# Moving transposes, a parameter copy and the skip term inside a fused state-space and gated feed-forward kernel

## The chip, the core and the metric

The kernel runs on one core of a Trainium2 chip. The metric is the device time of one execution in microseconds (us), the median of several runs. A core has a matrix engine (TensorE, PE in the profile), a vector engine (VectorE, DVE), a scalar engine (ScalarE, ACT), a general engine (GpSimd, POOL) and a queue engine that mainly issues transfers (SyncE, SP). SBUF is the on-chip memory; PSUM is the small memory into which TensorE writes.

## What is computed

Input x has 2048 tokens (rows) of 512 features. After a layer norm there are two branches. One is a linear recurrence over tokens with 512 complex states, plus a skip term `x * Dskip`; the other is a gated feed-forward network. The result joins them with x:

```python
xn = _layernorm(x)
# branch A: complex diagonal recurrence, 512 states
Lam_bar = exp(dt * Lam);  B_bar = ((Lam_bar - 1.0) / Lam)[:, None] * Bmat
Bu = einsum("bld,pd->blp", xn + 0j, B_bar)
h_t = Lam_bar * h_{t-1} + Bu_t                   # for each token t
s = 2.0 * einsum("blp,dp->bld", h, Cmat).real + xn * Dskip
# branch B: feed-forward, inner width 1376
g = silu((gelu(xn @ w_gate) * (xn @ w_up)) @ w_down)
return x + s * g
```

## The kernel before

The 2048 tokens are cut into four slabs (s = 0 to 3) of 512 tokens, and a slab into four tiles (m = 0 to 3) of 128. For TensorE, x must lie with its features on the partitions: this transposed, normalised x is `xnT`. For slab 0 it comes from TensorE transposes and VectorE copies, for the later slabs from a transposing transfer on the SP queue. The complex recurrence is turned into real scans by rotating with tables of cosines and sines (`cos_b`, `sin_b`), which the kernel builds from the parameters at the start.

The start, in program order. `BT` is B transposed, with ri = 0 the real and ri = 1 the imaginary half; `pv` holds the parameters as rows, `pf` as columns:

```python
def b_transposes(ri):
    for k0 in range(0, KT, 2):                       # KT = 4
        tb = psum.tile([P, 2, D], BF16, name="tb_ps", tag="ps")
        ... # 8 TensorE transposes of Bn into tb
        ACT(out=BT[:, ri, k0 : k0 + 2, :], in_=tb[:, :, :], func=AF.Copy)

dummies(12)                                          # matmuls on zeros, to wake the clock
b_transposes(0)
... # statistics of tiles 0..3 on VectorE; their power -0.5 on GpSimd
xs = [norm0(0), norm0(1)]                            # VectorE
tps = [t_xn0(0, xs[0]), t_xn0(1, xs[1])]             # 4 TensorE transposes each
nc.tensor.transpose(pt_ps[:, :], pv[:, :], ident[0:16, 0:16])
b_transposes(1)
nc.vector.tensor_copy(out=pf[:], in_=pt_ps[:, :])    # parameter copy
nc.gpsimd.tensor_tensor(out=dt_[:], in0=euler[:], in1=ldt, op=ALU.pow)
xs += [norm0(2), norm0(3)]
... # copy tps[0], tps[1] into xnT
tps += [t_xn0(2, xs[2]), t_xn0(3, xs[3])]
... # copy tps[2], tps[3] into xnT
... # angles from pf and dt_, sines on ScalarE, tables on VectorE
```

Each slab then has its input products `u_ps` (copied to `U` by ScalarE), a chain of rotations and scans on VectorE that gives `hst`, eleven feed-forward tiles (`ffn`), and four down products (`down`):

```python
def u_pair(s, h, first=None):                        # a pair of state tiles, h = 0, 1
    for q in range(H2):                              # H2 = 2
        for ri in range(2):
            ... # 4 matmuls over kt of BT[:, ri, kt, pt] and xnT into u_ps
            ACT(out=U[:, ri, q, :], in_=u_ps[:, :], func=AF.Copy)

def y_mm(s, m, hst):
    ... # 8 matmuls of hst and C2 into y_ps
    for kt in range(0 if (s, m) in zs else KT):      # skip term as 4 matmuls with diagI
        nc.tensor.matmul(y_ps[:, kt * P : (kt + 1) * P], lhsT=xnT[:, kt, mg : mg + P],
                         rhs=diagI[:, kt, :], start=False, stop=(kt == KT - 1))

def epi(s, m, y_ps, g2):
    def f():                                         # VectorE
        y = y_ps
        if (s, m) in zs:
            y = work.tile([P, D], FP32, name="yt", tag="tt", bufs=3)
            TT(out=y[:], in0=y_ps[:, :], in1=zs[s, m][:], op=ALU.add)
        TT(out=yg[:], in0=y[:, :], in1=g2[:], op=ALU.mult)
        TT(out=ot[:], in0=yg[:], in1=x_tok[:, s * M + m, :], op=ALU.add)
    dve(now() + 0.3, 0.95, f)
    nc.sync.dma_start(out=out_td[mg : mg + P, :], in_=ot[:])
```

`zs` holds, for the first three tiles of the last slab, the skip term already multiplied on VectorE. `ln_out` makes the normalised tile of the next slab, starts its transposing transfer, and for the last slab also that product:

```python
def ln_out(s, m):
    ACT(out=xn[:], in_=x_tok[:, s * M + m, :], func=AF.Identity, scale=..., bias=...)
    nc.sync.dma_start_transpose(out=xnT[:, :, c0 : c0 + P], in_=xn[:])
    if s == NS - 1 and m < M - 1:
        skip(s, m, xn, now() + 1.5)                  # z = xn * Db on VectorE
```

The last tile of all is written in two halves of 256 columns (`y_halves`). The order of the VectorE instructions is not the plain program order: the helpers `dve`, `later` and `flush` keep an estimated clock for TensorE and VectorE while the program is built, and put long VectorE work between the urgent pieces by it.

Of the kernel before, what the change touches and what calls it, by code (L numbers as in the profile page):

```python
# [10 lines left out]
AF = mybir.ActivationFunctionType  # L11
ALU = mybir.AluOpType
FP32 = mybir.dt.float32
BF16 = mybir.dt.bfloat16
# [5 lines left out]
def kernel(  # L20
# [17 lines left out]
    nc = tc.nc  # L38
    P = 128
    S = 2048  # L40
    D = 512
    F = 1376
    KT = D // P
    NPT = 4
    H2 = NPT // 2
    TS = 512
    NS = S // TS
    M = TS // P
# [7 lines left out]
    TT = nc.vector.tensor_tensor  # L56
    TSC = nc.vector.tensor_scalar
    STT = nc.vector.scalar_tensor_tensor
    ACT = nc.scalar.activation
# [4 lines left out]
    consts = ctx.enter_context(tc.tile_pool(name="consts", bufs=1))  # L64
    work = ctx.enter_context(tc.tile_pool(name="work", bufs=2))
    psum = ctx.enter_context(tc.tile_pool(name="psum", bufs=8, space=bass.MemoryType.PSUM))
# [7 lines left out]
    wu = consts.tile([P, KT, F], BF16, name="wu")  # L74
    wd = consts.tile([P, NFT, D], BF16, name="wd")
    BT = consts.tile([P, 2, KT, D], BF16, name="BT")
    Db = consts.tile([P, D], BF16, name="Db")
    C2 = consts.tile([P, 2, NPT, D], BF16, name="C2")
    pv = consts.tile([16, P], BF16, name="pv")
    at0 = work.tile([P, NFT, TS], BF16, name="at", tag="at")  # L80
    Bn = work.tile([P, 2, NPT, D], BF16, name="Bn", tag="at")
# [18 lines left out]
    for i, (a, b) in enumerate(zip(cuts[:-1], cuts[1:])):  # L100
        nc.sync.dma_start(out=wg[:, :, a:b], in_=wg_r[:, :, a:b])
        nc.sync.dma_start(out=wu[:, :, a:b], in_=wu_r[:, :, a:b])
        if i == 2:
            nc.sync.dma_start(out=Db[:], in_=A_Dskip.unsqueeze(0).to_broadcast([P, D]))
        if i == 0:
            nc.sync.dma_start(out=x_tok[:, M : 2 * M, :], in_=x_r[:, M : 2 * M, :])
    nc.sync.dma_start(
        out=wd[:, 0 : NFT - 1, :], in_=B_w_down[0 : (NFT - 1) * P, :].rearrange("(k p) d -> p k d", p=P)
# [10 lines left out]
    ident = consts.tile([P, P], BF16, name="ident")  # L119
# [10 lines left out]
    euler = consts.tile([P, NPT], FP32, name="euler")  # L130
# [6 lines left out]
    def dummies(n):  # L137
        w_ps = psum.tile([P, TS], FP32, name="w_ps", tag="ps")
        for _ in range(n):
            nc.tensor.matmul(w_ps[:, :], lhsT=warm[:, 0:P], rhs=warm[:], start=True, stop=True)  # L140

    def b_transposes(ri):
        for k0 in range(0, KT, 2):
            tb = psum.tile([P, 2, D], BF16, name="tb_ps", tag="ps")
            for k in range(2):
                for pt in range(NPT):
                    nc.tensor.transpose(
                        tb[:, k, pt * P : (pt + 1) * P], Bn[:, ri, pt, (k0 + k) * P : (k0 + k + 1) * P], ident[:]
                    )
            ACT(out=BT[:, ri, k0 : k0 + 2, :], in_=tb[:, :, :], func=AF.Copy)  # L150

    st = consts.tile([P, NS, M, 6], FP32, name="st")
    mv = consts.tile([P, NS, M, 2], FP32, name="mv")
# [21 lines left out]
    def t_xn0(m, xn):  # L175
        tp = psum.tile([P, KT, P], BF16, name="tp", tag="ps")
        for kt in range(KT):
            nc.tensor.transpose(tp[:, kt, :], xn[:, kt * P : (kt + 1) * P], ident[:])
        return tp

    pf = consts.tile([P, 16], FP32, name="pf")
# [6 lines left out]
    ch = consts.tile(W3, BF16, name="ch")  # L188


    dummies(12)
    b_transposes(0)
    for a in (0, 2):
        for m in (a, a + 1):
            bn(0, m)
# [4 lines left out]
    tps = [t_xn0(0, xs[0]), t_xn0(1, xs[1])]  # L200
    pt_ps = psum.tile([P, 16], BF16, name="pt_ps", tag="ps")
    nc.tensor.transpose(pt_ps[:, :], pv[:, :], ident[0:16, 0:16])
    b_transposes(1)
    nc.vector.tensor_copy(out=pf[:], in_=pt_ps[:, :])
    nc.gpsimd.tensor_tensor(out=dt_[:], in0=euler[:], in1=ldt, op=ALU.pow)
    xs += [norm0(2), norm0(3)]
    for m in range(2):
        nc.vector.tensor_copy(out=xnT[:, :, m * P : (m + 1) * P], in_=tps[m][:, :, :])
    tps += [t_xn0(2, xs[2]), t_xn0(3, xs[3])]
    for m in range(2, 4):  # L210
        nc.vector.tensor_copy(out=xnT[:, :, m * P : (m + 1) * P], in_=tps[m][:, :, :])
    STT(out=thn[:], in0=lim, scalar=1.0 / (2.0 * math.pi), in1=dt_[:], op0=ALU.mult, op1=ALU.mult)
    TT(out=a1[:], in0=lre, in1=dt_[:], op=ALU.mult)
    nc.gpsimd.tensor_tensor(out=rho[:], in0=euler[:], in1=a1[:], op=ALU.pow)
# [54 lines left out]
            TSC(out=diagI[:, kt, :], in0=ident_f[:], scalar1=dsk[:, kt : kt + 1], scalar2=None, op0=ALU.mult)  # L269

    def fold_c(pt):
        tA = work.tile([P, D], FP32, name="tA", tag="tt", bufs=3)
        tB = work.tile([P, D], FP32, name="tB", tag="tt", bufs=3)
        ACT(out=tA[:], in_=CT[:, 1, pt, :], func=AF.Copy, scale=cim[:, pt : pt + 1])
        ACT(out=tB[:], in_=CT[:, 0, pt, :], func=AF.Copy, scale=cim[:, pt : pt + 1])
        dve(now() + 0.8, 0.66, lambda: STT(
            out=C2[:, 0, pt, :], in0=CT[:, 0, pt, :], scalar=cre[:, pt : pt + 1], in1=tA[:],
            op0=ALU.mult, op1=ALU.subtract,
        ))
        dve(now() + 1.6, 0.66, lambda: STT(  # L280
            out=C2[:, 1, pt, :], in0=CT[:, 1, pt, :], scalar=ncre[:, pt : pt + 1], in1=tB[:],
            op0=ALU.mult, op1=ALU.subtract,
        ))
# [6 lines left out]
    def now():  # L290
        return clk["pe"]
# [17 lines left out]
    def dve(ready, cost, f, late=0.8):  # L309
        drain(ready, late)  # L310
        clk["dve"] = max(clk["dve"], ready) + cost
        f()
# [12 lines left out]
    def u_pair(s, h, first=None):  # L325
        cols = slice(s * TS, (s + 1) * TS)
        i = 2 * s + h - U_BUFS
        flush(("u", i // 2, i % 2))
        U = work.tile([P, 2, H2, TS], BF16, name="U", tag="U", bufs=U_BUFS)
        for q in range(H2):  # L330
            pt = h * H2 + q
            for ri in range(2):
                u_ps = psum.tile([P, TS], FP32, name="u_ps", tag="ps")
                for kt in range(KT):
                    nc.tensor.matmul(  # L335
                        u_ps[:, :], lhsT=BT[:, ri, kt, pt * P : (pt + 1) * P], rhs=xnT[:, kt, cols],
                        start=(kt == 0), stop=(kt == KT - 1),
                    )
                pe_takes(KT)
                ACT(out=U[:, ri, q, :], in_=u_ps[:, :], func=AF.Copy)  # L340
                if first is not None:
                    first()
                    first = None
        return U
# [103 lines left out]
    def y_mm(s, m, hst):  # L448
        m0 = m * P
        mg = s * TS + m0  # L450
        for h in range(2):
            flush(("h", s, h))
        y_ps = psum.tile([P, D], FP32, name="y_ps", tag="ps")
        for j in range(2 * NPT):
            nc.tensor.matmul(  # L455
                y_ps[:, :], lhsT=hst[:, j // NPT, j % NPT, m0 : m0 + P], rhs=C2[:, j // NPT, j % NPT, :],
                start=(j == 0), stop=((s, m) in zs and j == 2 * NPT - 1),
            )
        for kt in range(0 if (s, m) in zs else KT):
            nc.tensor.matmul(  # L460
                y_ps[:, kt * P : (kt + 1) * P], lhsT=xnT[:, kt, mg : mg + P], rhs=diagI[:, kt, :],
                start=False, stop=(kt == KT - 1),
            )
        pe_takes(2 * NPT + 1)
        return y_ps

    def epi(s, m, y_ps, g2):
        mg = s * TS + m * P
        yg = work.tile([P, D], BF16, name="yg", tag="yg")
        ot = work.tile([P, D], BF16, name="ot", tag="ot")  # L470

        def f():
            y = y_ps
            if (s, m) in zs:
                y = work.tile([P, D], FP32, name="yt", tag="tt", bufs=3)
                TT(out=y[:], in0=y_ps[:, :], in1=zs[s, m][:], op=ALU.add)  # L476
            TT(out=yg[:], in0=y[:, :], in1=g2[:], op=ALU.mult)
            TT(out=ot[:], in0=yg[:], in1=x_tok[:, s * M + m, :], op=ALU.add)

        dve(now() + 0.3, 0.95, f)  # L480
        nc.sync.dma_start(out=out_td[mg : mg + P, :], in_=ot[:])
# [21 lines left out]
            TT(out=ot[:, c], in0=yg[:, c], in1=x_tok[:, s * M + m, c], op=ALU.add)  # L503
            (nc.sync, nc.scalar)[i].dma_start(out=out_td[mg : mg + P, c], in_=ot[:, c])

    zs = {}

    def skip(s, m, xn, ready):
        zs[s, m] = work.tile([P, D], BF16, name="z", tag="z", bufs=3)
        dve(ready, 0.34, lambda: TT(out=zs[s, m][:], in0=xn[:], in1=Db[:], op=ALU.mult))  # L510


    sx = consts.tile([P, NS, 2, M], FP32, name="sx")
    mq = consts.tile([P, NS, M], FP32, name="mq")
# [18 lines left out]
    def ln_out(s, m):  # L533
        xn = work.tile([P, D], BF16, name="xn", tag="xn", bufs=4)
        ACT(out=xn[:], in_=x_tok[:, s * M + m, :], func=AF.Identity, scale=rs[:, s, m : m + 1], bias=nb[:, s, m : m + 1])  # L535
        c0 = s * TS + m * P
        nc.sync.dma_start_transpose(out=xnT[:, :, c0 : c0 + P], in_=xn[:])
        if s == NS - 1 and m < M - 1:
            skip(s, m, xn, now() + 1.5)


    for ri, src in enumerate((A_C_re, A_C_im)):
# [31 lines left out]
    for s in range(NS):  # L574
# [20 lines left out]
        if s < NS - 1:  # L595
# [4 lines left out]
            for m in range(M):  # L600
                g2s[s, m] = down(s, m, ats[s])
    s = NS - 1
    for m in range(M):
        g2s[s, m] = down(s, m, ats[s])
        if m > 0:
            epi(s, m - 1, y_mm(s, m - 1, hsts[s]), g2s[s, m - 1])
    y_halves(s, M - 1, hsts[s], g2s[s, M - 1])


# [28 lines left out]
```

## Time and profile before

The median of three runs is 190.83 us (190.41 to 191.14). The profiled execution has a span of 188.8 us. Cut into stages by the starts of the slabs' input products and of the last down products, it looks like this (busy us of each engine):

| stage, us from the start | length | PE | DVE | ACT |
|---|---|---|---|---|
| start, to the first input product: 0 to 10.55 | 10.55 | 7.65 | 6.52 | 4.83 |
| slab 0: 10.55 to 36.91 | 26.36 | 25.90 | 24.43 | 24.92 |
| slab 1: 36.91 to 80.30 | 43.39 | 43.18 | 39.83 | 31.55 |
| slab 2: 80.30 to 124.70 | 44.40 | 43.01 | 41.78 | 28.98 |
| slab 3, to its down products: 124.70 to 168.09 | 43.39 | 43.11 | 38.57 | 23.77 |
| the end: 168.09 to 188.80 | 20.71 | 16.62 | 7.79 | 2.43 |

(Down products and y of a slab lie partly in the next stage.) A time in the profile is counted from the start of the span. "L335" is line 335 of the kernel before. In a group or timeline line, "out<-in" names the tile written and the tiles read, xN is the number of instructions merged in the line, and a bracket at the end gives the idle time of that engine ahead of the instruction and what ended it. [...] consecutive matmuls overlap in the records: what counts is the distance between their starts.

### The profile page before, as it was taken

The numbers are of one execution on the slowest core, as the hardware profiler recorded it, in microseconds if no ns is written. First come the engines' busy times: TensorE is split into PE (matmuls) and PEld (weight loads), VectorE is DVE, ScalarE is ACT, GpSimd is POOL, SyncE is SP. The second block draws the span as 40 slices with busy tenths as digits, with TensorE's granted clock in tenths as the row PEclk, the third lists the DMA queues.
The fourth block names the chain that finished last, engine by engine and source line by source line (L and its number), as shares of the span: only waits on it lengthen the run. The fifth ranks groups of instructions, "written<-read, shape, count | busy, mean of one in ns | idle before, by whom it ended". The sixth has DMA issues, their size and how long they took to land.

```text
span 188.8 us, 2554 instructions
## 1 busy us (share of the span) xinstructions
PE 179.5 (95%) x888; PEld 85.4 (45%) x905; DVE 158.9 (84%) x275; ACT 116.5 (62%) x209; POOL 20.3 (11%) x35
## 2 busy tenths in 40 slices
PE   7789999999999999999999999979999999999991
PEld 2544444444444444544444444534444444444451
DVE  4699699999998599999999977999999999540544
ACT  3489999997269969257259939727529644352110
POOL 3567200000000340000000180000000000000000
PEclk9999999999999999999999999999999999999999
DMA  5999977700000013200000003111000000000001
GB/s 153 316 371 361 224 141 220 145 3 0 0 0 0 0 23 91 56 28 28 3 2 0 0 2 83 40 47 56 0 0 0 3 0 27 28 28 31 28 30 56
DMA packets 21292, 12.39 MB, mean 66 GB/s; under 512 B 11456, under 2 KB 21280, under 8 KB 21280
## 3 DMA queue, kind: packets, MB, share of 16 engines
q1 hardware_dynamic: 21104, 12.16, 23.8%
q8 instruction: 7, 0.11, 0.3%
q10 hardware_dynamic: 176, 0.07, 0.1%
q14 instruction: 5, 0.04, 0.1%
HBM read 7.51 MB, written 2.10 MB: 51 GB/s over the span
## 4 chain that ended last, share of the span: by engine, by line
PE 76%; DVE 8%; ACT 6%; DMA 6%; issue 1%; SPq 1%; DVEq 0%; ACTq 0%
PE f_ps L440 20%; PE g_ps L420 15%; PE up_ps L425 15%; PE y_ps L455 13%; PE u_ps L335 11%; DMA Bn<-in_A_B_im_dram 3%; DMA xnT<-xn 3%; ACT U L340 2%; PE y_ps L460 1%; DVE at L433 1%; ACT ca L323 1%; ACT ub L432 1%; DVE Wt L358 1%; ACT L430 1%; DVE t__256 L569 1%
## 5 line engine op out<-in xcount | busy, mean ns | idle before, releaser
L425 PE MATMUL up_ps<-xnT,wu 128*128 128x512 bf16 (+1 forms) x172 | 44.8, 379 | 0.3
L420 PE MATMUL g_ps<-xnT,wg 128*128 128x512 bf16 (+1 forms) x174 | 44.7, 379 | 0.1
L440 PE MATMUL f_ps<-wd,at 128*128 128x512 bf16 (+1 forms) x174 | 38.9, 379 | 0.2
L430 ACT ACTIVATE gt<-g_ps 128x512 bf16<-128x512 f32 (+1 forms) x44 | 26.0, 592 | 10.6 <-PE g_ps L420 8.2
L335 PE MATMUL u_ps<-xnT,BT 128*128 128x512 bf16 x124 | 27.9, 379 | 2.3 <-DMA xnT<-xn 1.5
L384 DVE TENSOR_TENSOR_SCAN Ft<-rho,it,Wt 128x512 bf16<-128x512 f32 x24 | 30.0, 1272 | 0.0
L432 ACT ACTIVATE ub<-up_ps 128x512 bf16<-128x512 f32 (+1 forms) x44 | 26.3, 597 | 4.1 <-PE up_ps L425 3.7
L455 PE MATMUL y_ps<-C,hst 128*128 128x512 bf16 x115 | 27.8, 379 | 0.2
L445 ACT ACTIVATE g<-f_ps 128x512 f32<-128x512 f32 x16 | 9.6, 597 | 28.6 <-PE f_ps L440 28.6
L425 PEld LDWEIGHTS <-wu 128*128 128x128 bf16 (+1 forms) x176 | 17.6, 100 | 20.4
L440 PEld LDWEIGHTS <-at 128*128 128x128 bf16 (+1 forms) x176 | 17.2, 98 | 20.6
L420 PEld LDWEIGHTS <-wg 128*128 128x128 bf16 (+1 forms) x176 | 17.2, 100 | 18.4
L340 ACT ACTIVATE U<-u_ps 128x512 bf16<-128x512 f32 x32 | 17.9, 600 | 9.9 <-PE u_ps L335 9.9
L433 DVE TENSOR_TENSOR at<-gt,ub 128x512 bf16<-128x512 bf16 (+1 forms) x44 | 18.1, 415 | 6.9 <-ACT ub L432 6.6
L335 PEld LDWEIGHTS <-BT 128*128 128x128 bf16 x128 | 12.3, 98 | 17.0 <-issue 2.1
L455 PEld LDWEIGHTS <-hst 128*128 128x128 bf16 x120 | 11.7, 98 | 14.1
L535 ACT ACTIVATE xn<-x_tok,nb,rs 128x512 bf16<-128x512 bf16 x12 | 9.7, 812 | 4.5 <-POOL nb L531 4.5
L525 POOL TENSOR_SCALAR sx<-sx 128x4 f32<-128x4 f32 x2 | 2.2, 1115 | 83.9 <-ACT junk L520 83.9
L358 DVE TENSOR_TENSOR Wt<-pp,qq 128x1024 bf16<-128x1024 bf16 x16 | 10.6, 688 | 0.3
L358 DVE TENSOR_TENSOR hst<-pp,qq 128x1024 bf16<-128x1024 bf16 x16 | 10.6, 687 | 0.2
L520 ACT ACTIVATE junk<-x_tok 128x512 bf16<-128x512 bf16 x16 | 10.1, 630 | 0.3
L476 DVE TENSOR_TENSOR yt<-y_ps,z 128x512 f32<-128x512 f32 x3 | 2.1, 691 | 9.7 <-PE y_ps L455 9.7
(112 smaller groups left out, 171.7 us busy)
## 6 DMA issues: line engine op xcount, KB each, us to landing
out_dram<-ot SPq DMA_DIRECT2D x15, 128.0 KB, 1.7
x_tok<-in_A_x_dram SPq DMA_DIRECT2D x3, 512.0 KB, 5.8
wd<-in_B_w_down_dram SPq DMA_DIRECT2D x1, 1280.0 KB, 11.0
Bn<-in_A_B_re_dram SPq DMA_DIRECT2D x1, 512.0 KB, 4.3
Bn<-in_A_B_im_dram SPq DMA_DIRECT2D x1, 512.0 KB
wg<-in_B_w_gate_dram SPq DMA_DIRECT2D x1, 512.0 KB
wu<-in_B_w_up_dram SPq DMA_DIRECT2D x1, 512.0 KB, 8.4
wg<-in_B_w_gate_dram SPq DMA_DIRECT2D x1, 480.0 KB
```

The source lines that it names most:

```text
L335: nc.tensor.matmul(u_ps[:, :], lhsT=BT[:, ri, kt, pt * P : (pt + 1) * P], rhs=xnT[:, kt, cols], start=(kt == 0), stop=(kt == KT - 1),)
L340: ACT(out=U[:, ri, q, :], in_=u_ps[:, :], func=AF.Copy)
L358: return lambda: TT(out=dst()[i], in0=box["pp"][:, i, :, :], in1=box["qq"][:, 1 - i, :, :], op=op)
L384: nc.vector.tensor_tensor_scan(out=box["F"][:, ri, q, :], data0=rho[:, pt : pt + 1].to_broadcast([P, TS]), data1=box["W"][:, ri, q, :], in ...
L420: nc.tensor.matmul(g_ps[:fs, :], lhsT=wg[:, kt, fsl], rhs=xnT[:, kt, cols], start=(kt == 0), stop=(kt == KT - 1))
L425: nc.tensor.matmul(u_ps[:fs, :], lhsT=wu[:, kt, fsl], rhs=xnT[:, kt, cols], start=(kt == 0), stop=(kt == KT - 1))
L430: ACT(out=gt[:fs], in_=g_ps[:fs, :], func=AF.Gelu_apprx_tanh)
L432: ACT(out=ub[:fs], in_=u_ps[:fs, :], func=AF.Copy)
L433: dve(now() + 0.9, 0.34, lambda: TT(out=at[:fs, j, :], in0=gt[:fs], in1=ub[:fs], op=ALU.mult))
L440: nc.tensor.matmul(f_ps[:, :], lhsT=at[:fs, k, m0 : m0 + P], rhs=wd[:fs, k, :], start=(k == 0), stop=(k == NFT - 1))
L455: nc.tensor.matmul(y_ps[:, :], lhsT=hst[:, j // NPT, j % NPT, m0 : m0 + P], rhs=C2[:, j // NPT, j % NPT, :], start=(j == 0), stop=((s, m) ...
L520: ACT(out=junk[:], in_=x_tok[:, s * M + m, :], func=f, accum_out=sx[:, s, i, m : m + 1])
```

## The change

The change does five things. B's imaginary half is transposed in two parts around the transposes of the second half of x, so that x is not queued behind all of it. In each pair of input products, both real ones come first, so that the imaginary half of `BT` is needed later. On VectorE the norms of tiles 2 and 3 and the copies into `xnT` go ahead of the parameter copy. Ten dummy matmuls stand in place of twelve. And the VectorE version of the skip term in the last slab is taken out: its products `z`, its additions `yt` and the load of `Db` go, and all tiles use the four TensorE products with `diagI`. With that, y of the last slab's tile 0 is put ahead of the four down products, tiles 1 and 2 behind them, and the two temporaries `tA` and `tB` of the folding of C get two buffers each in place of three shared ones.

```diff
-        if i == 2:
-            nc.sync.dma_start(out=Db[:], in_=A_Dskip.unsqueeze(0).to_broadcast([P, D]))
...
-    dummies(12)
-    b_transposes(0)
+    dummies(10)
+    b_transposes(0, 0)
+    b_transposes(0, 2)
...
     nc.tensor.transpose(pt_ps[:, :], pv[:, :], ident[0:16, 0:16])
-    b_transposes(1)
-    nc.vector.tensor_copy(out=pf[:], in_=pt_ps[:, :])
-    nc.gpsimd.tensor_tensor(out=dt_[:], in0=euler[:], in1=ldt, op=ALU.pow)
     xs += [norm0(2), norm0(3)]
     for m in range(2):
         nc.vector.tensor_copy(out=xnT[:, :, m * P : (m + 1) * P], in_=tps[m][:, :, :])
+    b_transposes(1, 0)
     tps += [t_xn0(2, xs[2]), t_xn0(3, xs[3])]
+    b_transposes(1, 2)
     for m in range(2, 4):
         nc.vector.tensor_copy(out=xnT[:, :, m * P : (m + 1) * P], in_=tps[m][:, :, :])
+    nc.vector.tensor_copy(out=pf[:], in_=pt_ps[:, :])
+    nc.gpsimd.tensor_tensor(out=dt_[:], in0=euler[:], in1=ldt, op=ALU.pow)
...
-        tA = work.tile([P, D], FP32, name="tA", tag="tt", bufs=3)
-        tB = work.tile([P, D], FP32, name="tB", tag="tt", bufs=3)
+        tA = work.tile([P, D], FP32, name="tA", tag="tA")
+        tB = work.tile([P, D], FP32, name="tB", tag="tB")
...
-        for q in range(H2):
-            pt = h * H2 + q
-            for ri in range(2):
+        for ri in range(2):
+            for q in range(H2):
+                pt = h * H2 + q
...
-        for kt in range(0 if (s, m) in zs else KT):
+        for kt in range(KT):
...
-            y = y_ps
-            if (s, m) in zs:
-                y = work.tile([P, D], FP32, name="yt", tag="tt", bufs=3)
-                TT(out=y[:], in0=y_ps[:, :], in1=zs[s, m][:], op=ALU.add)
-            TT(out=yg[:], in0=y[:, :], in1=g2[:], op=ALU.mult)
+            TT(out=yg[:], in0=y_ps[:, :], in1=g2[:], op=ALU.mult)
...
-        if s == NS - 1 and m < M - 1:
-            skip(s, m, xn, now() + 1.5)
...
     s = NS - 1
+    y0 = y_mm(s, 0, hsts[s])
     for m in range(M):
         g2s[s, m] = down(s, m, ats[s])
-        if m > 0:
-            epi(s, m - 1, y_mm(s, m - 1, hsts[s]), g2s[s, m - 1])
+        if m == 0:
+            epi(s, 0, y0, g2s[s, 0])
+    for m in range(1, M - 1):
+        epi(s, m, y_mm(s, m, hsts[s]), g2s[s, m])
     y_halves(s, M - 1, hsts[s], g2s[s, M - 1])
```

Putting the VectorE orders of the two programs side by side shows one more difference: around the wait ahead of slab 3, one product `at` (gate times up) now stands behind the first scan of its chain instead of ahead of it, and near the change from slab 2 to slab 3 the `yg` and `ot` of two tiles change places with the small carry operations and with a rotation product.

More of the change, by code (lines that the diff above doesn't have):

```diff
@@ L76 @@
     BT = consts.tile([P, 2, KT, D], BF16, name="BT")
-    Db = consts.tile([P, D], BF16, name="Db")
     C2 = consts.tile([P, 2, NPT, D], BF16, name="C2")
@@ L140, in dummies, with b_transposes @@
             nc.tensor.matmul(w_ps[:, :], lhsT=warm[:, 0:P], rhs=warm[:], start=True, stop=True)
[L142 to L150, printed above, removed]
+    def b_transposes(ri, k0):
+        tb = psum.tile([P, 2, D], BF16, name="tb_ps", tag="ps")
+        for k in range(2):
+            for pt in range(NPT):
+                nc.tensor.transpose(
+                    tb[:, k, pt * P : (pt + 1) * P], Bn[:, ri, pt, (k0 + k) * P : (k0 + k + 1) * P], ident[:]
+                )
+        ACT(out=BT[:, ri, k0 : k0 + 2, :], in_=tb[:, :, :], func=AF.Copy)
     st = consts.tile([P, NS, M, 6], FP32, name="st")
@@ L456, in y_mm @@
                 y_ps[:, :], lhsT=hst[:, j // NPT, j % NPT, m0 : m0 + P], rhs=C2[:, j // NPT, j % NPT, :],
-                start=(j == 0), stop=((s, m) in zs and j == 2 * NPT - 1),
+                start=(j == 0), stop=False,
             )
-        for kt in range(0 if (s, m) in zs else KT):
+        for kt in range(KT):
             nc.tensor.matmul(
@@ L504, in y_halves @@
             (nc.sync, nc.scalar)[i].dma_start(out=out_td[mg : mg + P, c], in_=ot[:, c])
[L506 to L510, printed above, removed]
     sx = consts.tile([P, NS, 2, M], FP32, name="sx")
```

## The prediction

> **What bounds the kernel now.** I read the page's busy table first, then the list of what TensorE (PE) waited for, then the chain that ended last, then the timeline of the four places where that list or the chain shows a gap.
>
> ```profile
> PE 179.5 (95%) x888; PEld 85.4 (45%) x905; DVE 158.9 (84%) x275; ACT 116.5 (62%) x209; POOL 20.3 (11%) x35
> ```
>
> ```profile
> PE u_ps L335 <- DMA xnT<-xn: 1.5, 2, 1.2
> PE w_ps L140 <- DVE halfpi L116: 1.2, 1, 1.2
> PE tb_ps L147 <- DMA Bn<-in_A_B_re_dram: 0.9, 1, 0.9
> PE u_ps L335 <- DVE xnT L211: 0.6, 1, 0.6
> PE tb_ps L147 <- DMA Bn<-in_A_B_im_dram: 0.2, 1, 0.2
> ```
>
> The numbers after the colon are total us, times, longest. TensorE is busy 95% of 188.8 us and its waits add to 4.4 us. Between 10.55 us, when the first real product starts, and 184.76 us, when the last matmul ends, only the first row (1.5 us) is idle. So the change can win only at the start, at the two waits for transposed x, and after the last matmul, or lose by giving TensorE more matmuls.
>
> The start, with columns start, duration, engine, instruction:
>
> ```profile
> 8.00 0.18 PE L202 MATMUL pt_ps<-ident,pv 16*128 16x16 bf16 x1
> 8.21 0.17 DVE L204 CAST pf<-pt_ps 128x16 f32<-128x16 bf16 x1 [1.39 <-PE pt_ps L202]
> 8.30 0.73 DVE L169 TENSOR_SCALAR xn<-x_tok,mv,rs 128x512 bf16<-128x512 bf16 x2
> 8.41 1.07 PE L147 MATMUL tb_ps<-ident,Bn 128*128 128x128 bf16 x16 [0.23 <-DMA Bn<-in_A_B_im_dram]
> 9.31 0.61 PE L178 MATMUL tp<-ident,xn 128*128 128x128 bf16 x8
> 9.74 0.76 DVE L211 COPY xnT<-tp 128x512 bf16<-128x512 bf16 x2
> 10.55 5.77 PE L335 MATMUL u_ps<-xnT,BT 128*128 128x512 bf16 x25 [0.62 <-DVE xnT L211]
> ```
>
> VectorE (DVE) idles 1.39 us before the tiny parameter copy; TensorE does 16 transposes of B_im before the second half of x; the first product waits 0.62 us for the last copy into xnT.
>
> The wait before slab 1 (the first row is the chain's: start, duration, what):
>
> ```profile
> 34.18 2.69 DMA xnT<-xn
> 36.91 6.87 PE L335 MATMUL u_ps<-xnT,BT 128*128 128x512 bf16 x31 [0.31 <-DMA xnT<-xn]
> ```
>
> The wait before slab 3:
>
> ```profile
> 120.59 0.67 DVE L477 TENSOR_TENSOR yg<-y_ps,g 128x512 bf16<-128x512 f32 x1
> 121.29 0.42 DVE L478 TENSOR_TENSOR ot<-yg,x_tok 128x512 bf16<-128x512 bf16 x1
> 121.74 0.33 SPq L481 DMA_DIRECT2D out_dram<-ot  x1
> 122.16 1.20 SPq L537 DMA_TRANSPOSE xnT<-xn  x1
> 124.72 2.53 PE L335 MATMUL u_ps<-xnT,BT 128*128 128x512 bf16 x10 [1.20 <-DMA xnT<-xn]
> ```
>
> The queue is in order: the last transpose of x stands behind an output store, and the store behind VectorE. The end:
>
> ```profile
> 182.83 0.69 DVE L476 TENSOR_TENSOR yt<-y_ps,z 128x512 f32<-128x512 f32 x1 [2.16 <-PE y_ps L455]
> 183.62 0.69 DVE L477 TENSOR_TENSOR yg<-yt,g 128x512 bf16<-128x512 f32 x1
> 184.35 0.43 DVE L478 TENSOR_TENSOR ot<-yg,x_tok 128x512 bf16<-128x512 bf16 x1
> 184.69 0.42 DVE L502 TENSOR_TENSOR yg<-y_ps,g 128x256 bf16<-128x256 f32 x1
> 185.80 0.29 DVE L503 TENSOR_TENSOR ot<-yg,x_tok 128x256 bf16<-128x256 bf16 x1
> ```
>
> [...] four 128-column skip products take 0.22 us, eight 512-column ones 1.73 us. [...] Here dummies are 0.43 us apart until 4.56 us (3.4 us after the first), then closer. [...] yt and yg measure 691 and 690. [...]
>
> **The change part by part.**
>
> *Start.* VectorE now does norms 2 and 3 straight after 0 and 1. Their scale comes from GpSimd at about 7.05 us (6.26 + 0.79), so both end near 7.8 instead of 9.03. TensorE still waits until 8.41 for B_im (no transfer before it changes), does 8 transposes (half of the 0.90 us from 8.41 to 9.31: 0.45), then x tiles 2 and 3 from 8.86 rather than 9.31, then the other 8, done at 9.76. The copies move with x, from 9.74 to 9.29, and the first product from 10.55 to about **10.10: 0.45 us**. The second half of B_im still reaches ScalarE (ACT) before it finishes the earlier copies, so its four, of 0.95 us, still end at 11.0. Real products first means that B_im is wanted only at 10.10 + 2 × 0.86 = 11.8, so it holds nothing. Ten dummies instead of twelve end about 0.43 us (2 × 0.215) before the old end, but the next transposes wait for B_re at 6.55 anyway: 0.
>
> *What it pushes back.* The parameter copy now follows the xnT copies. It goes from 8.21 to about 10.05, GpSimd's power (1.05 us) ends near 11.3, and the angles start at 11.45 instead of 10.60: the sines, U and the rotation tables come 0.85 us later. TensorE is not held: the PSUM buffer of the first gate product (17.45) was emptied at 13.5, and ScalarE, late by 0.85, has caught up by the fourth feed-forward tile, since at 22.83 to 24.56 it waits for TensorE. VectorE is late too, but waits for ScalarE at 36 to 40 us (about 0.6 in sum, from the starts there) and 0.48 at 58.9; its hst of slab 0, done at 62.27, has 1.6 us before y at 63.87. Cost 0.
>
> *Slab 1.* TensorE would arrive at 36.60 − 0.45 = 36.15, but xnT lands at 36.87. Its queue has been full since the loads: four transposes 1.3 us apart start at 30.15 though their xn were ready from 25.85. Removing the Db load takes 128 KB from that queue, at 361 GB/s (8 to 20 us) 0.36 us; its issue lasted 1.40 us, but beside other full transfers, so I take 0.4. Then xnT lands near 36.5 and slab 1 starts **0.4 us** earlier; the head's 0.45 is not added to this, it only turns into waiting. If the whole 1.40 counts, TensorE's own 0.75 is the limit.
>
> *Slab 3.* Three z products (0.34 us start to start) leave VectorE's queue. The first only used idle time. From qq at 115.59 the rest run: two Wt, one at, then the scan at 118.46 instead of 119.39; the moved at follows at 119.7, yg at 120.06, ot ends near 121.15 instead of 121.71. The transpose is issued about 0.53 us earlier in relation to TensorE, and the wait falls from 1.20 to 0.67: **0.53 us**.
>
> *End.* Three y groups get their four skip products back: 12 × 0.054 = **0.65 us more** TensorE. From the last full y (T = 182.79 before) VectorE took 0.79 + 0.73 + 0.34 and two half pairs to 186.09, T + 3.30. Now yg starts at T + 0.04, ot at 0.77, the first half at 1.11, but the second half's matmuls end only at T + 1.97, so it runs 2.03 to 2.77: **0.53 saved**. Loss 0.12. Putting y of tile 0 ahead of the down products moves work of the same size; at of the last tile (ready 167.3) has time.
>
> Sum: 0.40 + 0.53 − 0.12 = 0.81 us. 190.83 − 0.8 = **190.0 us**.
>
> **Rivals.** (a) *Only the sums of work count*: TensorE gets 0.65 more and the waits come back elsewhere. For it: TensorE at 95% and slab 1's wait eating the head's gain. Against it: the slab 3 wait is VectorE's order, which does change. It makes 191.3. (b) *The parameter delay reaches TensorE*: ScalarE and VectorE are both nearly full from 21 to 57 us. For it: 0.85 us of delay in engines with little air. Against it: 1.6 us of margin at y and a PSUM margin of over 3 us. If half of it got through, 190.4. (c) *The queue gains the full 1.4 us* from Db: 189.6. (d) *Cold clock*: ten dummies end near 5.25 us (5.68 − 0.43), leaving 1.3 us idle rather than 0.87. [...] the transposes run at half rate and the start loses about 0.9 us (16 × 56 ns): 190.9. Against it: the rate had already risen at about 4.6 us, after eight dummies (3.4 / 0.43).
>
> **Range and chances.** (c) sets the low side with a better slab 3 (the wait wholly gone, 0.7 more): 189.2. (b) and (d) set the upper side: 190.8. The three runs of before spread 0.7 us, so the centre is itself uncertain by 0.3. A 2% change is 3.8 us; all of TensorE's waits are 4.4, of which 2.1 for data on its way at the start stay. So both outer chances are small.
>
> **What would show it.** Right: the first u_ps at about 10.1 us; VectorE without the 1.39 us idle; angles 0.85 us later; slab 1's u_ps at 36.5 with a wait of 0.3 to 0.4 still there; slab 3's wait at 0.6 to 0.7; three fewer yt and z; the last VectorE operation 0.8 us after the last matmul ends instead of 1.3. Wrong: dummies at half rate to the end and slow transposes after them; a wait of y for hst or of g_ps for ScalarE; a slab 1 wait above 0.5; TensorE's sum not up by 0.65 at the end.

## The result, and the profile after

| | median, us | runs |
|---|---|---|
| before | 190.62 | 4 (190.41 to 191.14) |
| after | 188.50 | 4 (188.29 to 189.05) |

The ratio is 0.9889, with a 95% interval of 0.9857 to 0.9921: 2.1 us faster, where 0.8 had been predicted. The span went from 188.8 to 186.5 us. TensorE's work is the same to 0.2 us (twelve skip products more, two dummies fewer); VectorE has six instructions and 3.4 us less. The engines' row of the page after:

```profile
PE 179.7 (96%) x898; PEld 85.9 (46%) x915; DVE 155.5 (83%) x269; ACT 115.5 (62%) x209; POOL 21.4 (11%) x35
```

What TensorE waited for after the change, the same list as before (total us, times, longest):

```profile
PE w_ps L137 <- DVE halfpi L113: 1.2, 1, 1.2
PE tb_ps L143 <- DMA Bn<-in_A_B_re_dram: 0.8, 1, 0.8
PE tb_ps L143 <- DMA Bn<-in_A_B_im_dram: 0.4, 1, 0.4
PE u_ps L333 <- DVE xnT L207: 0.2, 1, 0.2
```

The row of 1.5 us that stood first, the two waits for transposed x, is gone whole. What is left lies ahead of the first product. From that product to the last matmul nothing in this list holds TensorE.

The start in the timeline after (start, duration, engine, line, instruction, idle time ahead):

```profile
8.40 0.62 PE L143 MATMUL tb_ps<-ident,Bn 128*128 128x128 bf16 x8 [0.35 <-DMA Bn<-in_A_B_im_dram]
8.86 0.61 PE L174 MATMUL tp<-ident,xn 128*128 128x128 bf16 x8
9.28 0.76 DVE L207 COPY xnT<-tp 128x512 bf16<-128x512 bf16 x2 [0.76 <-PE tp L174]
9.95 0.16 DVE L208 CAST pf<-pt_ps 128x16 f32<-128x16 bf16 x1
10.09 1.67 PE L333 MATMUL u_ps<-xnT,BT 128*128 128x512 bf16 x6 [0.18 <-DVE xnT L207]
```

Eight transposes of B, then x, then (not shown) the other eight, which now fill the time in which VectorE copies. The first product is at 10.09 us.

Where the 2.1 us came from is read by lining up the starts of the slabs' input products in the two traces:

| start of | before | after | earlier by | new in this stage |
|---|---|---|---|---|
| slab 0, first product | 10.55 | 10.09 | 0.46 | 0.46 |
| slab 1 | 36.91 | 35.98 | 0.93 | 0.47 |
| slab 2 | 80.14 | 79.20 | 0.94 | 0.01 |
| slab 3 | 124.72 | 122.42 | 2.30 | 1.36 |
| last `ot` on VectorE | 185.80 | 183.63 | 2.17 | −0.13 |

So the largest piece, 1.36 us, is gained right before slab 3, and the end loses 0.13. These are two single profiles: the piece of slab 1 differs from profile to profile, as shown below. (In the profile of before, slab 2 starts at 80.14 and the last down products at 167.93; the stage table above was cut at 80.30 and 168.09.)

### The profile page after: what moved, and what is told of

Same layout as the page of the kernel before. It is cut to its first block, busy times and chain, and to the rows that moved or that the text cites. A ratio compares the mean times of both kernels' runs of the same rounds, so it can differ in the third digit from the quotient of the medians.

```text
span 186.5 us, 2568 instructions
## 1 busy us (share of the span) xinstructions
PE 179.7 (96%) x898; PEld 85.9 (46%) x915; DVE 155.5 (83%) x269; ACT 115.5 (62%) x209; POOL 21.4 (11%) x35
## 4 chain that ended last, share of the span: by engine, by line
PE 93%; DMA 3%; SPq 1%; DVE 1%; issue 1%
PE f_ps L438 20%; PE up_ps L423 20%; PE g_ps L418 20%; PE u_ps L333 15%; PE y_ps L453 14%; DMA Bn<-in_A_B_im_dram 3%; PE y_ps L458 2%; PE y_ps L486 1%; DVE xnT L207 0%; PE tb_ps L143 0%; SPq L93 0%; SPq L89 0%; DVE yg L496 0%; SPq L92 0%; SPq L91 0%
## 5 line engine op out<-in xcount | busy, mean ns | idle before, releaser
L428 ACT ACTIVATE gt<-g_ps 128x512 bf16<-128x512 f32 (+1 forms) x44 | 26.6, 604 | 9.8 <-PE g_ps L418 7.5
L430 ACT ACTIVATE ub<-up_ps 128x512 bf16<-128x512 f32 (+1 forms) x44 | 26.8, 609 | 3.4 <-PE up_ps L423 2.9
L471 DVE TENSOR_TENSOR yg<-y_ps,g 128x512 bf16<-128x512 f32 x15 | 10.2, 683 | 13.7 <-PE y_ps L458 9.9
```

What stands on the lines that cost most here:

```text
L428: ACT(out=gt[:fs], in_=g_ps[:fs, :], func=AF.Gelu_apprx_tanh)
L430: ACT(out=ub[:fs], in_=u_ps[:fs, :], func=AF.Copy)
L471: TT(out=yg[:], in0=y_ps[:, :], in1=g2[:], op=ALU.mult)
```

## The experiments

**Two halves of the change.** The first pair splits the change. One kernel has only the skip term's part: no `z`, `yt` or `Db`, the new places of y in the last slab, and the two buffers each for `tA` and `tB`; its start is the old one. The other has only the new start and the real-first order of a pair.

```diff
 # skip term only: the kernel after, with the start of before
-    dummies(10)
+    dummies(12)
...  # B's imaginary half in one piece, parameter copy ahead of norms 2 and 3, q outside ri
```

> The kernel before with only the skip part of the change (no Db load, no z, no yt, y of the last slab moved, tA and tB with two buffers), the start left as it was. Theory (the gain is two removed waits for transposed x, both due to the skip term): first input product at 10.55 us as before, no wait ahead of slab 1 (TensorE's own limit 36.60), no wait ahead of slab 3, about 1.7 us faster than before. Rival (the head's 0.46 us is part of the gain and simply adds): about the same 1.7, so this run has to be read with the next one. Second rival (only the sums of work count): 0.65 us slower than before.

Measured: 189.33 us, ratio 0.9928 (0.9899 to 0.9958). In its trace the first product is at 10.83, slab 1 starts at 36.73, slab 3 at 123.16, neither with a wait.

```diff
 # new start only: the kernel before, with the start of after
-    dummies(12)
+    dummies(10)
...  # B's imaginary half in two pieces, parameter copy last, ri outside q
```

> The kernel before with only the start changed (transposes of B split, parameter copy later, real products first, ten dummies); Db, z and yt stay. Theory: the first input product at 10.09 us, but the wait ahead of slab 1 grows from 0.31 to about 0.77, slab 1 still starts at 36.9, the wait ahead of slab 3 stays at 1.2; the time is within 0.1 us of before. Rival (gains add): 0.46 us faster. Rival (the later parameters reach TensorE): up to 0.4 us slower.

Measured: 190.64 us, ratio 1.0004 (0.9986 to 1.0021). The wait ahead of slab 3 is still 1.2 us. (Its profile caught B landing late, with 2.0 us of waiting for it, and, after sixteen transposes at the usual distance of 0.056 us, others 0.107 us apart, so that the first product came at 11.80; the times are of 20 runs.) So two thirds of the gain belong to the skip term, about 0.7% or 1.4 us, and the new start alone brings nothing that shows. The product of the two ratios is 0.9932, short of the whole 0.9889, but each of the three has an interval of 0.002 to 0.003 either way, so the gap may be noise. Whether something in the two helps only together is taken up below.

**The wait ahead of slab 3.** The prediction gave it 0.53 us. The two traces show why it is more. VectorE before:

```profile
114.19 0.42 DVE L510 TENSOR_TENSOR z<-xn,Db 128x512 bf16<-128x512 bf16 x1 [2.03 <-ACT xn L535]
114.53 0.68 DVE L477 TENSOR_TENSOR yg<-y_ps,g 128x512 bf16<-128x512 f32 x1
```

and after:

```profile
111.12 0.68 DVE L471 TENSOR_TENSOR yg<-y_ps,g 128x512 bf16<-128x512 f32 x1
115.33 0.43 DVE L431 TENSOR_TENSOR at<-gt,ub 128x512 bf16<-128x512 bf16 x1 [1.21 <-ACT ub L430]
117.79 0.68 DVE L471 TENSOR_TENSOR yg<-y_ps,g 128x512 bf16<-128x512 f32 x1
```

Before, VectorE stood idle 2.03 us with `z` at the head of its queue, waiting for ScalarE's `xn`, while the `yg` behind it had all it needed: its y had left TensorE at about 109.0 us, and the last of ScalarE's gates ahead of it had ended at 97.4. In this trace the queue keeps its order: the ready `yg` starts at 114.53, 0.34 us after `z`, not before it. The norms of tiles 2 and 3 at the start of before show the same: their scale is there at 7.05, and they start at 8.30, behind the parameter copy at 8.21. After, that `yg` runs at 111.12. The SP queue keeps its order too: before, the last transpose, whose `xn` ScalarE had ended at 119.17, is issued at 122.16, behind the store at 121.74. On the SP queue that feeds slab 3, and on TensorE, this gives, after:

```profile
118.98 0.54 SPq L475 DMA_DIRECT2D out_dram<-ot  x1
119.61 1.19 SPq L525 DMA_TRANSPOSE xnT<-xn  x1
...
122.42 3.83 PE L333 MATMUL u_ps<-xnT,BT 128*128 128x512 bf16 x16
```

The last transpose is issued at 119.61 rather than 122.16, and `u_ps` follows y without a wait.

My first theory was narrow: the first `z` alone, with its 2.03 us, is the cause. The rival was that all three count. Two kernels take opposite parts out.

```diff
 # all but the first z
-        if s == NS - 1 and m < M - 1:
+        if s == NS - 1 and 0 < m < M - 1:
```

> The kernel before, but z and yt only for tiles 1 and 2 of the last slab; tile 0 uses the four TensorE products. Theory (the first z stands at the head of VectorE's queue waiting for xn while a finished yg is behind it): the 2.03 us of idle ahead of z are gone, the yg of tile 0 of slab 2 runs at about 112 instead of 114.5, and the wait ahead of slab 3 falls from 1.2 to under 0.3; about 1 us faster than before. Rival (what counts is the VectorE time of the z products, 0.34 us each): the wait falls by at most 0.4, to 0.8 or more.

Measured: 190.79 us, ratio 0.9997 (0.9973 to 1.002). Its VectorE and TensorE around the place:

```profile
115.74 0.42 DVE L433 TENSOR_TENSOR at<-gt,ub 128x512 bf16<-128x512 bf16 x1 [1.21 <-ACT ub L432]
...
119.66 0.66 DVE L477 TENSOR_TENSOR yg<-y_ps,g 128x512 bf16<-128x512 f32 x1
...
123.79 2.53 PE L335 MATMUL u_ps<-xnT,BT 128*128 128x512 bf16 x11 [0.81 <-DMA xnT<-xn]
```

The narrow theory fell. The 2.03 us are gone from the head of the queue, but 1.21 us come back as a wait of `at` for ScalarE, and the two `z` that are left still stand between that `at` and the second `yg`, the one whose store is ahead of the transpose; around them VectorE idles for ScalarE twice more, 0.31 and 0.28 us.

```diff
 # the first z only
-        if s == NS - 1 and m < M - 1:
+        if s == NS - 1 and m == 0:
```

> The kernel before with z and yt for tile 0 of the last slab only; tiles 1 and 2 use the TensorE products. Theory (the first z holds the queue): the idle of 2 us ahead of z stays, the yg of slab 2's tile 0 still runs at about 114.5, and the wait ahead of slab 3 only falls by the time of two z and the at that moves (about 0.5 of 1.3), to 0.8. Rival (each z costs its own time): the same kernel shows the wait at 0.4 or less, as two of three z are gone.

Measured: 190.27 us, ratio 0.9951 (0.9929 to 0.9973); the first `z` idles its 2.03 us as before, and TensorE waits 0.55:

```profile
113.83 0.43 DVE L510 TENSOR_TENSOR z<-xn,Db 128x512 bf16<-128x512 bf16 x1 [2.03 <-ACT xn L535]
...
123.70 1.67 PE L335 MATMUL u_ps<-xnT,BT 128*128 128x512 bf16 x7 [0.55 <-DMA xnT<-xn]
```

So taking out either part alone leaves a wait. The third kernel keeps everything, `z`, `yt` and `Db`, and only moves the three `z` to a time in slab 3 when VectorE has air:

```diff
 # z late
-            skip(s, m, xn, now() + 1.5)
+            held.append((m, xn))
...
+                if s == NS - 1 and j == 8:               # in slab 3, its ninth feed-forward tile
+                    for m, xn in held:
+                        skip(s, m, xn, now())
```

> The kernel before with all three z products kept, but put into VectorE's queue later, behind the eighth feed-forward tile of slab 3, where VectorE has idle time; all else, the Db load and yt too, is as before. Theory (only the place of z in the queue matters): the idle of 2.0 us ahead of the first z is gone, the wait ahead of slab 3 is 0, the time falls by about 1.4 us, as in the run of the skip part alone (1.3). Rival (the VectorE time of z and yt, the Db load or the end of the kernel matter): half of that or less.

Measured: 189.80 us, ratio 0.9934 (0.991 to 0.9959). From its trace:

```profile
119.12 0.68 DVE L477 TENSOR_TENSOR yg<-y_ps,g 128x512 bf16<-128x512 f32 x1
...
123.73 2.54 PE L335 MATMUL u_ps<-xnT,BT 128*128 128x512 bf16 x11
```

No wait ahead of slab 3, with all the work still there. It is the place of `z` in the queue that cost the time. The whole skip part brought no more (0.9928), so nothing that shows is left for `yt`, the load of `Db`, the new places of y and the buffers of `tA` and `tB`. (This profile has a wait of 0.84 us ahead of slab 1, which is taken up below.) The five kernels side by side, in us from the start of the last y of slab 2 on TensorE (121.40 before, 120.47 after):

| kernel | second `yg` | last transpose issued | `u_ps` of slab 3 |
|---|---|---|---|
| before | −0.81 | 0.76 | 3.32 |
| all but the first `z` | −1.20 | 0.37 | 2.93 |
| first `z` only | −1.48 | 0.10 | 2.66 |
| `z` late | −2.66 | −0.84 | 1.95 |
| after | −2.68 | −0.86 | 1.95 |

1.95 us is what y itself takes on TensorE (eight products 0.216 us apart and four 0.056 apart, with records of 0.38 and 0.22 us), so the last two rows are the floor. A time can lag its row for a plain reason: without the first `z`, tile 0 gets its four skip products back on TensorE (0.22 us), so that of 0.39 us only 0.17 should be left, within the interval.

**The wait ahead of slab 1.** This is about the `Db` load in the SP queue. Its 4 + 4 transposes of C and 4 of x, before (start, duration of the group on the queue):

```profile
16.04 7.61 SPq L544 DMA_TRANSPOSE CT<-in_A_C_re_dram  x4
...
30.15 5.25 SPq L537 DMA_TRANSPOSE xnT<-xn  x4
```

and after:

```profile
15.70 6.57 SPq L530 DMA_TRANSPOSE CT<-in_A_C_re_dram  x4
...
28.77 5.21 SPq L525 DMA_TRANSPOSE xnT<-xn  x4
```

The queue reaches C 0.34 us earlier, as the bytes had said, but the four transposes of C that follow the loads take another 1.04 us less; x comes 1.38 us earlier. To see whether `Db` does this, it was put back into the kernel after:

```diff
+        if i == 2:
+            nc.sync.dma_start(out=Db[:], in_=A_Dskip.unsqueeze(0).to_broadcast([P, D]))
```

> The changed kernel with the load of Db put back in its old place; its tile is read by nobody. Theory (that one load costs the transfer queue 1.4 us ahead of the transposes of x): first transpose of x at about 30.15 instead of 28.77, slab 1 starts at 36.9 instead of 35.98 with a wait of about 0.8, slab 3 without a wait; 0.9 us slower than the changed kernel. Rival of the prediction (the load costs its bytes only, 0.36 us, and the rest came from elsewhere): the transpose at 29.1, slab 1 starts at 35.98, no difference.

Measured: 188.92 us, ratio 0.992 (0.9899 to 0.994). The first transpose of x goes from 28.77 to 29.65, 0.88 us later, and yet its trace shows no wait at slab 1 (start 36.17). The time is 0.3% above that of after, with overlapping intervals. So in this pair `Db` costs the queue about 0.9 us, and slab 1 lists no wait either way. The other profiles show how unsteady both numbers are. The first transpose of x for slab 1 is issued at, in us:

| | `Db` early | without `Db`, or `Db` late |
|---|---|---|
| old start | 29.61 to 30.15 (4 profiles) | 29.43, 29.45 |
| new start | 29.65 to 29.93 (3 profiles) | 28.77 to 28.99 (5 profiles) |

With the old start `Db` costs 0.2 to 0.7 us, with the new one 0.7 to 1.2; why the start matters to the queue stays open. Of the seven profiles with `Db` early, two list a wait ahead of slab 1: before, with 0.31, and `z` late:

```profile
37.29 7.08 PE L335 MATMUL u_ps<-xnT,BT 128*128 128x512 bf16 x32 [0.84 <-DMA xnT<-xn]
```

There the first transpose was issued at 29.76, earlier than in before, and x still landed later. (A third, the first `z` only, loses 0.16 us there by the distance between starts.) Of the seven without `Db` or with it late, none waits. Three more kernels make a square of it: new start (here with twelve dummies) or old, `Db` early or behind slab 1's transposes.

```diff
 # Db late
-        if i == 2:
-            nc.sync.dma_start(out=Db[:], in_=A_Dskip.unsqueeze(0).to_broadcast([P, D]))
...
+                if j == 7:                               # in slab 0, after slab 1's last transpose
+                    nc.sync.dma_start(out=Db[:], in_=A_Dskip.unsqueeze(0).to_broadcast([P, D]))
```

New start, `Db` early:

> The kernel before with the new start, but twelve dummies; Db in its old place, z and yt as before. Theory (Db holds back the transposes of x, so that the earlier start becomes a wait ahead of slab 1): 0.1 to 0.2 us faster than before, slab 1 no earlier than about 36.3 with a wait ahead of it. Rival (the half clock of ten dummies ate the gain of the start): 0.45 us faster than before, no such wait.

Old start, `Db` late:

> The kernel before with only the Db load moved behind the transposing transfers for slab 1. Theory: no wait ahead of slab 1, which starts 26.4 - 0.3 to 0.5 = about 25.9 us after the first input product; 0.2 to 0.3 us faster than before. Rival (the load costs nothing): the same as before.

New start, `Db` late ("the run before this one" is the one with the new start and `Db` early):

> The kernel of the run before this one with the Db load moved behind the transposing transfers for slab 1. Theory: the first of these transfers starts at about 28.8 instead of 29.7, no wait ahead of slab 1, and the start's 0.46 us and slab 1's wait both come through: 0.6 us faster than before. Rival (the load costs nothing): the same as the run before this one.

| ratio to before | `Db` early | `Db` late |
|---|---|---|
| old start | 1 | 0.9989 (0.9975 to 1.0004) |
| new start | 0.9995 (0.9978 to 1.0012) | 0.9969 (0.9948 to 0.999) |

Only the corner with both has an interval clear of 1, 0.31% or 0.6 us (only its times are used: its profile has a span of 388.4 us). The theory behind the square was that the later of two conditions decides: slab 1 starts when TensorE has done slab 0, 25.9 us after the first product, and when the last transposed x has landed. The square does not show that the two gains need each other: 0.9995 times 0.9989 is 0.9984, inside the interval of the corner with both, so that gains that merely add fit as well. And the wait expected with the new start and `Db` early is not in its profile, whose first product came late, at 10.90:

```profile
36.80 6.85 PE L336 MATMUL u_ps<-xnT,BT 128*128 128x512 bf16 x31
```

The sum of the whole change closes either way: 0.9934 for `z` late times 0.9969 for the new start with `Db` late is 0.9903, within the interval of 0.9889.

**The start.** The kernel after was run again, and beside it with twelve dummies.

```diff
-    dummies(10)
+    dummies(12)
```

> The changed kernel once more, unaltered, with more rounds. Theory (the first profile's two gains were a wait ahead of slab 3 of 1.4 us, which is in every run of before, and one ahead of slab 1 of 0.3 us, which is in some of its runs only, beside 0.46 at the start): 1.8 us faster than before, median about 188.8; no wait ahead of slabs 1 and 3 in the profile. Rival (the 2.1 us of the first four runs hold): median 188.5. With ten dummies a run in ten shows a clock of 0.99 and is about 1.2 us longer.

> The changed kernel with twelve dummies again. Theory [...]: no run at a clock of 0.992 or less, the slowest runs near 189.6 rather than 190.3, the median the same within 0.2 us. Rival (two dummies cost their time, 0.43 us): 0.4 us slower. Rival (nothing depends on them): runs at 0.99 are as frequent as with ten.

Measured: 188.88 us, 0.9889 (0.9867 to 0.991), with ten and 188.85 us, 0.9888 (0.9861 to 0.9916), with twelve: no difference. But the profile with ten, of the very same kernel, happened to catch the slow transposes of rival (d):

```profile
6.38 1.89 PE L143 MATMUL tb_ps<-ident,Bn 128*128 128x128 bf16 x16 [0.76 <-DMA Bn<-in_A_B_re_dram]
```

Sixteen transposes in 1.89 us, against 1.07 in the first profile of it, after an idle time that was no longer (0.76 against 0.80). The next eight of B took 1.03 instead of 0.62, and the first product came at 11.33 instead of 10.09. So two profiles of one kernel have 1.24 us between their first products, and no run here shows why. The record of the granted clock reads 1.00 here, so that the half rate is read from the distances alone (0.107 us against 0.056); in the profile of the new start alone, which has the same distances, it reads 0.57 on the mean from 8 to 12 us, and 1.00 in the 4 us before and after. Twelve dummies do not exclude it: the first four transposes in one such profile (copy early, below) and the first seven in another (new start, `Db` early) are 0.1 us apart. That is two of four profiles with ten dummies and two of twelve with twelve, too few to say whether ten make it more frequent. In the times, four of the 43 runs with ten dummies (4, 20, 13 and 6 of four sets) have a clock of 0.988 to 0.991 and are 1.0 to 1.4 us above their set's median; with twelve such runs come too: two runs of the 59 of before read 0.987 and 0.991 and are 1.6 and 1.9 us above.

Two kernels, each with twelve dummies and profiled once, undo one piece of the start. First the parameter copy back ahead of norms 2 and 3, then B's imaginary half in one piece ahead of x:

```diff
 # copy early
+    nc.vector.tensor_copy(out=pf[:], in_=pt_ps[:, :])
+    nc.gpsimd.tensor_tensor(out=dt_[:], in0=euler[:], in1=ldt, op=ALU.pow)
     xs += [norm0(2), norm0(3)]
```

> The changed kernel with twelve dummies, and with the parameter copy and the power after it put back ahead of the norms of tiles 2 and 3. To be read from the first transpose of the imaginary half of B, which a load releases, to the first input product: 2.14 us before, 1.69 in the changed kernel with twelve dummies. Theory (VectorE's in-order queue waits with the norms behind the copy): the idle of about 1.4 us ahead of the copy comes back, the copies into xnT are pushed back, and the stretch is about 2.0 us. Rival (only the split of the transposes matters): 1.7 us.

```diff
 # B's imaginary half whole
     b_transposes(1, 0)
+    b_transposes(1, 2)
     tps += [t_xn0(2, xs[2]), t_xn0(3, xs[3])]
-    b_transposes(1, 2)
```

> The changed kernel with twelve dummies, and with all 16 transposes of the imaginary half of B ahead of the second half of x again; the parameter copy stays late. Theory (x waits in TensorE's queue for the second eight transposes, 8 x 56 ns): the stretch from the first transpose of that half to the first input product is 2.14 us as before, against 1.69 with the split. Rival (the late copy alone gives the gain): 1.7 us.

B lands at different times in different runs (in the eight profiles in which TensorE waits for its imaginary half, the first transpose of it starts at 8.34 to 9.21 us), so the stretch from the first transpose of its imaginary half to the first product is compared: 2.14 us before, 1.69 after (8.40 to 10.09), 1.69 with twelve dummies, 1.82 with the copy early, 2.13 with B whole. Without the split, the late copy brings nothing (2.13 against 2.14); without the late copy, the split brings 0.32 of the 0.45. The copy, with 0.94 us of idle VectorE ahead of it, costs only 0.13 in this profile, since the norms behind it were done almost in time.

**A version that beats both.** What was learnt gives two more kernels. The first takes x's transposes wholly ahead of B's imaginary half, and sends the loads of x for slabs 2 and 3 behind slab 1's transposes:

```diff
-    b_transposes(1, 0)
     tps += [t_xn0(2, xs[2]), t_xn0(3, xs[3])]
+    b_transposes(1, 0)
     b_transposes(1, 2)
...
-    for s in range(2, NS):
-        nc.sync.dma_start(out=x_tok[:, s * M : (s + 1) * M, :], in_=x_r[:, s * M : (s + 1) * M, :])
...
+                if j == 7:                               # in slab 0
+                    ... # the two loads of x_tok
```

> The changed kernel with twelve dummies, all transposes of x ahead of the imaginary half of B, and the loads of x for slabs 2 and 3 behind the transposing transfers for slab 1. Theory (x is ready from 7.8 us and only stands behind B; the imaginary half is needed two product groups later): the first input product at about 9.4 us or 0.7 us earlier than with the split, no wait ahead of slab 1, 0.7 us faster than the changed kernel, ratio to before about 0.985. Rival (the gain turns into a wait for the imaginary half on ScalarE or for transposed x): under 0.3 us.

Measured: 188.18 us, ratio 0.9875 (0.984 to 0.9909). From its timeline:

```profile
8.84 1.06 PE L143 MATMUL tb_ps<-ident,Bn 128*128 128x128 bf16 x16
9.73 1.46 PE L333 MATMUL u_ps<-xnT,BT 128*128 128x512 bf16 x5
```

The first product is at 9.73, with no wait ahead of it and no wait for B's imaginary half; slab 1 follows at 35.63. The time alone does not set it apart from the kernel after (0.9889). The second kernel adds the skip term of tiles 0 and 1 on VectorE again, but with `z` in slab 3's idle time and `Db` late:

```diff
+        if s == NS - 1 and m < 2:
+            held.append(xn)
...
+                if s == NS - 1 and j == 8:
+                    ... # z = xn * Db for the two tiles; y of these without diagI, with yt
```

> The kernel of the run before this one, with the skip term of the last slab's tiles 0 and 1 on VectorE again, the products z in its idle time of slab 3 and the Db load behind all other loads. Theory (TensorE is busy throughout, so eight of its 128-column products less are 8 x 54 ns = 0.43 us, and z in idle time costs nothing): 0.4 us faster than that run, no wait ahead of slab 3. Rival (yt delays the last outputs or z comes in the way again): no gain or a loss.

Measured: 187.78 us, ratio 0.9836 (0.9807 to 0.9864). All six of its times (187.06 to 188.17) lie below all ten of the kernel after in its two sets (188.29 to 189.56). In its profile a wait of 0.5 us ahead of slab 3 is back: the last transpose of x took 2.09 us on the queue there instead of 1.2. Why was not tried.

## Why the prediction was wrong, point by point

- **The start was right, in this pair of profiles.** 0.45 us was worked out, 0.46 measured; half of B's transposes and the copies that follow x are in the timeline as described, and the kernel with B whole gives the gain back. Luck had a part: two of the four profiles with ten dummies have slow transposes and a first product at 11.33 and 11.80. The angles start at 11.50 instead of 10.60, 0.90 against 0.85 expected, and TensorE is held nowhere for it, as said.
- **The end was right.** A loss of 0.12 was worked out. From the start of slab 3 to the last `ot` it is 61.08 us before and 61.21 after: 0.13. VectorE's last operation ends 0.78 us after the last matmul (184.76 and 186.09 before, 183.14 and 183.92 after, with the records' ends), where 0.8 had been said.
- **Slab 1 was too small by half.** The prediction let the start's 0.45 turn into waiting and gave 0.40 for the removal of `Db`, with a wait of 0.3 to 0.4 remaining. In the two profiles 0.93 came through, 0.46 of the start and 0.47 of wait, and no wait remained. The wait had been read too small: the list counts 0.31 from the end of the last record of slab 0, but from that matmul's start to `u_ps` it is 0.69 us, where 0.22 is usual, so 0.47 was lost. The load was mis-sized too: 0.36 to 0.4 by its bytes, 0.88 of queue with the new start (28.77 against 29.65). That lies towards rival (c), which had been given as the low side. But with `Db` put back slab 1 did not wait either, and among the four profiles with the old start and `Db` early, before has the last first transpose (29.61 to 30.15). So one profile's wait was taken as a fixed property, and how much of the 0.47 the change brings on the mean stays open.
- **Slab 3 was the step that failed.** "The first only used idle time" was the sentence. It is true of VectorE and wrong of the queue: the idle time was spent with a ready `yg` behind the `z`. The prediction then moved everything from `qq` on by the work removed, and got 0.53 us. In fact `qq` itself came 2.5 us earlier in relation to TensorE (115.59 to 112.18, less the 0.93 by which all is earlier), part of it was lost again to the wait for `ub`, and 1.87 remained for the second `yg`. That is more than the wait had, so that the gain was the whole 1.37 us between y and `u_ps`.
- **The rivals.** (a) and (b) did not come: TensorE's added work at the end is paid back within 0.13 us, and the parameter delay reaches nothing (y of slab 0 starts at 63.70 before, not 63.87, so that its margin was 1.4 rather than 1.6 us; it was enough). (d): slow transposes do happen, 0.107 us apart, but that ten dummies bring them is not shown, and twelve instead of ten change no time that shows (188.85 against 188.88). The argument against it, that the rate rises at 4.6 us (0.43 us between dummies until 4.56, 0.215 from 4.87), was one profile's: in all four profiles with ten dummies these stay 0.43 us apart to the last.

With 0.46, 0.47, 1.36 and −0.13 the sum is 2.16 us, where 0.81 was expected; slab 3 makes 0.83 of the difference, and the start and slab 1 together 0.53 (0.93 against the 0.40 that had been left of them). The total does not hang on the two profiles, since the second set of times gives the same 0.9889; the split between start and slab 1 does.

## What to carry to other kernels

Before an engine's idle time is called free, look at what stands behind the instruction that waits: if the next one was ready, the whole wait is on its path, as here, where a `yg` with its y done at 109.0 stood behind the 2.03 us of `z` and started at 114.53. When such a blocker is taken out, look for the next wait that takes its place, and move all that stands between it and the urgent work; here moving was enough, and the work could stay. And where an engine's arrival meets a landing transfer, as at slab 1, one profile shows only which came last that time (the transposes of x began at 29.61 to 30.15 in four profiles that share the old start and the early `Db`): read several before giving such a wait a size.

## What the runs showed of the hardware

- With the new start, a load of 128 KB in the SP queue delayed what stood behind it by about 0.9 us (29.65 against 28.77), more than the 0.36 us that its bytes would take, an estimate from the 361 GB/s that before moved from 8 to 20 us: 0.50 at the start of the first transposes of C (16.20 against 15.70) and 0.37 in these four themselves (6.94 against 6.57). With the old start it was 0.2 to 0.7 us.
- The same kernel, with the same ten dummies and nearly the same idle time after them, took 1.07 or 1.89 us for its first sixteen transposes, and in the second case its transposes stayed slow, 0.107 us apart against 0.056, until about 10 us.
